# Two heads-blocks transposed by DMA instead of TensorE, later visits of the second batch, and a re-use of the score buffers, in a fused sigmoid-attention and ReGLU kernel

## The chip, the cores and the metric

The kernel runs on one core of one Trainium2 chip. The metric is the device time in microseconds (us). A core has TensorE (PE; its weight loads are listed apart as PEld), VectorE (DVE), ScalarE (ACT), GpSimd (POOL) and SyncE (SP), and 16 DMA engines that all transfers share. TensorE's results go to PSUM, eight banks of 2 KB in each of 128 partitions; VectorE and ScalarE take them from there into SBUF. Each engine works through its own instructions in order, and waits on semaphores for the others.

## What is computed

Sigmoid attention over 8 batches, 12 heads, 448 positions and 64 values a head, then a feed-forward layer (FFN) with a gate, from 768 to 1536 and back. All is float32 at the borders.

```python
scores = scale * np.matmul(q, k.transpose(0, 1, 3, 2)) - np.log(S)
attn = 1.0 / (1.0 + np.exp(-scores))
x = np.matmul(attn, v).transpose(0, 2, 1, 3).reshape(B * S, H * D)
gate = np.maximum(x @ w_gate, 0.0)
out = (gate * (x @ w_val)) @ w_out
```

## The kernel before

**Blocks and passes.** Four heads of one batch form a block; there are three blocks a batch and 24 in all (n = 0 to 23). A block's keys are cut into seven chunks of 64. One chunk of one block is a pass (168 passes): `scores` issues four matmuls of 64x64 by 448 into a PSUM tile of two banks, and one sigmoid on ScalarE turns that into `PT` (line 181). `values` then sums the seven chunks of a block against v into another two-bank tile (line 195), and two evictions make two `xT` tiles of it, VectorE's (line 211) for block 0, 1 and the first half of 2, ScalarE's (line 209) for the others. Six xT tiles are one batch's input to the FFN.

**FFN.** For each batch, `up` (twelve times) takes six matmuls for the gate and six for the value (line 230); VectorE applies the ReLU into `gate_sb` (line 247) and multiplies into `hT` (line 254). `down` (line 269) takes 128 rows of the result at a time, a part of 512 and a part of 256 columns, twelve matmuls each; VectorE scales them into `ysb` (line 283), and SyncE stores them (line 289). The first batch has three blocks of 128 rows. In the very last block, the second part is cut once more into two halves of 128 columns, in two PSUM tiles, evicted by ScalarE and VectorE.

**PSUM.** Two pools: `qkp`, three tiles of two banks, for scores, for values and for some transposes, and `wkp`, two tiles of one bank, for gate, value and down, for other transposes, and for the fillers. Fillers are matmuls with zeros at the start. They go into `fill` tiles of `wkp` (line 357).

**How q and k become operands.** They are loaded in float32, 128 rows by 896 values a block, cast to fp16 (line 105), and transposed. There are three routes. Blocks 0 to 3 go over TensorE into a `wkp` tile and over VectorE into `kT` and `qT` (line 163). Blocks 4 and 5 go the same way through a `qkp` tile (line 154); `feed` calls that after the fifth chunk (c == 4) of the block before. Blocks 6 to 23 are transposed by DMA, issued by SyncE (line 144): k, then q. The pool of kT and qT tiles has four, so that a block's tiles take the place of those of two blocks earlier.

**Who casts.** VectorE and ScalarE cast q and k of block 0, VectorE those of blocks 1 to 3, GpSimd all later ones (q first, then k, then v), and every v; GpSimd also casts the weights (line 137).

**The order of the work.** It is written out by hand. The program's order is each engine's order. A prologue runs passes 0 to 20 (batch 0). Loads that are not for blocks 0 to 2 come from one list, `order`. `start_next` takes the next item, issues its load on SyncE and its cast on GpSimd. Items are halves of the weights (g for the gate, u for the value, o for the output, three groups each) and the blocks 3, 4 and 5. Two items are taken before the passes, one in each pass from 11 to 20, and the others one at every eighth step of the first FFN. A weight load waits until one of five staging buffers has been cast.

In the FFN of batch b the passes of batch b+1 are dealt out as visits of three. The loop adds up the planned time of each step of `ffn` (0.189 us for an up matmul, columns/2400 + 0.002 for a down matmul); `todo` holds the times at which visits fall due, evenly spaced from `lo` to the end. There are eight visits in the first FFN, seven in the others. A visit issues its three passes; where a block's sigmoids are complete, it issues the values of that block ahead of its third pass; then `feed` is called for each pass. For blocks from 6 on, `feed` issues the casts at the block's predecessor's first chunk, and at its fourth chunk the DMA transposes and the load of the block after.

```python
if todo and t >= todo[0]:
    todo.pop(0)
    visit()
```

Of the kernel before, what the change touches and what calls it, by code (L numbers as in the profile page):

```python
# [9 lines left out]
FP32 = mybir.dt.float32  # L10
# [6 lines left out]
def kernel(  # L17
# [10 lines left out]
    nc = tc.nc  # L28
# [3 lines left out]
    P = 128  # L32
    HB = 4
    NBLK = H // HB
    NB = B * NBLK
    KC = 64
    NCH = S // KC
# [47 lines left out]
    def load_block(n: int, *which):  # L85
        b, i = divmod(n, NBLK)
        for nm, src, c0, c1, eng in which:
            st = stp.tile([P, 2, S], FP32, tag="st", name=f"st_{nm}")
            rows = src[b, i * HB : (i + 1) * HB].rearrange("(r h) (p c) d -> (h p) r (c d)", h=2, c=NCH)
            eng.dma_start(st[:, :, c0 * D : c1 * D], rows[:, :, c0 * D : c1 * D])  # L90
            staged[nm, n] = st

    def load_all(n: int):
        load_block(n, ("k", k, 0, NCH, nc.sync), ("q", q, 0, NCH, nc.sync), ("v", v, 0, NCH, nc.sync))

    def cast_qk(n: int, nm: str, *engines, cut=(0, NCH)):
        st = staged.pop((nm, n))
# [87 lines left out]
            qkT.pop(("k", n))  # L185

    def values(n: int, chunks):
        if chunks[0] == 0:
            PT[n] = qkp.tile([P, 2, 512], FP32, tag="qk", name="pv_ps")
        pv = PT[n]  # L190
        t = v16[n]
        for c in chunks:
            pt = PT.pop((n, c))
            for pr, r, o in ((0, 0, 0), (0, 64, 64), (1, 64, 0), (1, 0, 64)):
                nc.tensor.matmul(  # L195
                    pv[o : o + 64, pr, 0:S],
                    t[r : r + 64, pr, c * D : (c + 1) * D],
                    pt[r : r + 64, pr, :],
                    start=(c == 0),
                    stop=(c == NCH - 1),  # L200
                    tile_position=(r, o),
                    skip_group_check=True,
                )
        if chunks[-1] == NCH - 1:
            b, i = divmod(n, NBLK)
            for pr in range(2):
                x = xTp.tile([P, S], FP16, tag="xT", name="xT")
                if n >= NBLK or (pr and n == NBLK - 1):
                    nc.scalar.activation(x[:], pv[:, pr, 0:S], AF.Copy, scale=XSCALE)  # L209
                else:  # L210
                    nc.vector.tensor_scalar(  # L211
                        out=x[:], in0=pv[:, pr, 0:S], scalar1=XSCALE, scalar2=None, op0=AOP.mult
                    )
                xT[b, 2 * i + pr] = x
            PT.pop(n)
            v16.pop(n)
# [40 lines left out]
    def down(col0: int):  # L257
        o = col0 % (NHALF * S)
        ysb = ysbp.tile([P, DM], FP32, tag="ysb", name="ysb")
        last = col0 + P == B * S  # L260
        for m0, mn in ((0, 512), (512, DM - 512)):

            nb = 2 if last and m0 else 1
            w = mn // nb
            ys = [wkp.tile([P, 512], FP32, tag="wk", name="y_ps") for _ in range(nb)]
            for f in range(NFC):
                for j, y in enumerate(ys):
                    c0 = m0 + j * w
                    nc.tensor.matmul(  # L269
                        y[:, 0:w],  # L270
                        hT[f][:, o : o + P],
                        wo[f // FG][:, f % FG, c0 : c0 + w],
                        start=(f == 0),
                        stop=(f == NFC - 1),
                    )
                if f < NFC - 1:
                    yield mn / 2400.0 + 0.002
            for j, y in enumerate(ys):
                dst = ysb[:, m0 + j * w : m0 + (j + 1) * w]
                if nb == 2 and j == 0:  # L280
                    nc.scalar.activation(dst, y[:, 0:w], AF.Copy, scale=OUT_SCALE)  # L281
                else:
                    nc.vector.tensor_scalar(out=dst, in0=y[:, 0:w], scalar1=OUT_SCALE, scalar2=None, op0=AOP.mult)  # L283
            if last or m0 + mn == DM:
                s0 = m0 if last else 0
                for half, eng in enumerate((nc.sync, nc.scalar if last else nc.sync)):
                    b, r = divmod(col0 + 64 * half, S)
                    rows = out[b * S : (b + 1) * S].rearrange("(p c) m -> c p m", c=NCH)
                    eng.dma_start(rows[r // KC][:, s0 : m0 + mn], ysb[64 * half : 64 * half + 64, s0 : m0 + mn])
            yield mn / 2400.0 + 0.002  # L290
# [5 lines left out]
    def ffn(b: int):  # L296
        for f in range(NFC):
            if b == 0 and f == 0:
                yield from up(b, f, 4, 4)
            else:  # L300
                yield from up(b, f)
        for col0 in blocks128(b):
            yield from down(col0)
# [12 lines left out]
    def feed(i: int):  # L316

        n, c = divmod(i, NCH)
        m = n + 1
        if c == 0 and NPRO <= m < NB:  # L320
            cast_block(m)
        if c == 4 and NBLK < m < NPRO:
            transposes(m, "k")
            transposes(m, "q")
        if c == 3 and NPRO <= m < NB:
            dma_transposes(m)
        if c == 3 and NPRO <= m + 1 < NB:
            load_all(m + 1)

    valued: set = set()  # L330
    state = {"pass": NBLK * NCH}
    def visit():
# [16 lines left out]

    zeros = const.tile([P, 512], FP16, name="zeros")  # L350
    nc.vector.memset(zeros[:], 0.0)
    fill: list = []

    def filler(*widths):

        for w in widths:
            nc.tensor.matmul(fill[-1][:, 0:w], zeros[:, 0:P], zeros[:, 0:w], start=True, stop=True)

    def new_fill():
        fill.append(wkp.tile([P, 512], FP32, tag="wk", name="fill"))  # L360

    with tc.manual_schedule():
        nc.scalar.activation(warm[:], bias_t[:], AF.Sigmoid)  # L363
# [6 lines left out]
        def halves(kind, j):  # L370
            return [(kind, j, 0), (kind, j, 1)]

        order = halves("g", 0) + [3] + halves("u", 0) + halves("g", 1) + halves("u", 1)
        order += [4] + halves("g", 2) + halves("u", 2) + halves("o", 0) + [5]
        order += halves("o", 1) + halves("o", 2)

        def start_next():
            what = order.pop(0)
            if isinstance(what, int):
                load_all(what)  # L380
                if what > NBLK:
                    cast_block(what)
                else:
                    cast_v(what, nc.gpsimd)
            else:
                load_w(*what)
                cast_w(*what, nc.gpsimd)

        new_fill()
        filler(*[512] * 10)  # L390
        cast_qk(0, "q", nc.vector, nc.scalar, cut=(0, 4, NCH))
        cast_qk(0, "k", nc.vector, nc.scalar, cut=(0, 2, 4))
        transposes(0, "q")
        filler(128, 128)
        transposes(0, "k", nc.scalar, nc.vector, cut=(0, 2, 4))
        new_fill()
        filler(128, 128, 128)
        cast_qk(0, "k2", nc.vector, cut=(4, NCH))
        for n in range(NBLK):
# [7 lines left out]
        for i in range(NP0 + 2):  # L407
            n, c = divmod(i, NCH)
            if n < NBLK:
                scores(n, c)  # L410
            while done <= i - (4 if i < NP0 - 4 else 2):
                values(done // NCH, [done % NCH])
                done += 1
            if i == 2:
                qk16["k", 0] = qk16.pop(("k2", 0))
                transposes(0, "k", nc.vector, cut=(4, NCH))
            if 1 <= i <= 3:
                filler(256)
            if c == 1 and n + 1 < NBLK:
                cast_qk(n + 1, "k", nc.vector)  # L420
                cast_qk(n + 1, "q", nc.vector)
            if c in (3, 5) and n + 1 < NBLK:
                transposes(n + 1, "k" if c == 3 else "q")
            if i == 14:
                cast_qk(NBLK, "k", nc.vector)
            if i == 15:
                transposes(NBLK, "k")
                cast_qk(NBLK, "q", nc.vector)
            if i == 16:
                transposes(NBLK, "q")  # L430
            if i in (18, 21):
                gv_part(0, 0, wg, [0, 1] if i == 18 else [2, 3])
            if 11 <= i < NP0:
                start_next()

        for b in range(B):
            total = ffn_us(b)
            todo = []
            if b + 1 < B:
                count = NBLK * NCH // 3 + (1 if b == 0 else 0)  # L440
                lo = 6.0 if b == 0 else 0.0
                todo = [lo + (k + 0.5) * (total - lo) / count for k in range(count)]
            t = 0.0
            for step, cost in enumerate(ffn(b)):
                t += cost
                if order and step % 8 == 0:
                    start_next()
                if todo and t >= todo[0]:
                    todo.pop(0)
                    visit()  # L450
            for _ in todo:
                visit()

# [28 lines left out]
```

## Time and profile before

| what | value |
|---|---|
| median of 8 runs | 433.89 us (433.37 to 435.44) |
| the profiled execution | 434.65 us |
| its span, first to last instruction | 432.9 us |
| TensorE matmul busy | 418.9 us, 97% |
| VectorE / ScalarE / GpSimd busy | 166.0 / 178.7 / 103.2 us |
| up matmuls (line 230), 1152 | 254.9 us |
| down matmuls (line 269), 684 | 113.8 us |
| scores (line 171) and values (line 195), 672 each | 49.1 and 39.3 us |
| transposes on TensorE (line 157), 84 | 7.5 us |
| DMA transposes (line 144), 36 | 3.0 to 3.1 us from issue to landing |
| DMA, mean over the span | 155 GB/s |

Times in the profile are us from the start of the span. A row of a group gives the busy time, the mean of one in ns, and the idle time ahead of it with what ended it. Matmuls are pipelined and their ends are modelled, so that neighbours overlap in the records; the distance between starts is the better measure. The span leaves out 1.75 us that the execution's time includes.

### The profile page before, as it was taken

The numbers are of one execution on the slowest core, as the hardware profiler recorded it, in microseconds if no ns is written. First come the engines' busy times: TensorE is split into PE (matmuls) and PEld (weight loads), VectorE is DVE, ScalarE is ACT, GpSimd is POOL, SyncE is SP. The second block draws the span as 40 slices with busy tenths as digits, with TensorE's granted clock in tenths as the row PEclk, the third lists the DMA queues.
The fourth block names the chain that finished last, engine by engine and source line by source line (L and its number), as shares of the span: only waits on it lengthen the run. The fifth ranks groups of instructions, "written<-read, shape, count | busy, mean of one in ns | idle before, by whom it ended". The sixth has DMA issues, their size and how long they took to land.

```text
span 432.9 us, 7873 instructions
## 1 busy us (share of the span) xinstructions
PE 418.9 (97%) x3282; PEld 216.2 (50%) x3282; DVE 166.0 (38%) x276; ACT 178.7 (41%) x217; POOL 103.2 (24%) x137
## 2 busy tenths in 40 slices
PE   6879899999999999999999999999999999999996
PEld 3334455545455455554455454554455544555553
DVE  3535442244323533243522444234432445235531
ACT  5862445553534353525254435252534352500000
POOL 2667783233110333003230133103330030000000
PEclk9899999999999999999999999999999999999998
DMA  8999997365624754296432765156454630030014
GB/s 305 383 386 385 392 355 196 83 180 164 171 74 102 184 151 148 75 186 192 99 110 73 207 171 170 47 110 183 135 151 111 156 94 0 18 94 0 2 36 109
DMA packets 64371, 66.96 MB, mean 155 GB/s; under 512 B 35792, under 2 KB 54608, under 8 KB 64336
## 3 DMA queue, kind: packets, MB, share of 16 engines
q1 hardware_dynamic: 63088, 64.63, 51.4%
q10 hardware_dynamic: 1248, 1.84, 1.2%
q8 instruction: 25, 0.41, 0.4%
q14 instruction: 10, 0.08, 0.1%
HBM read 47.19 MB, written 11.01 MB: 134 GB/s over the span
## 4 chain that ended last, share of the span: by engine, by line
PE 92%; ACT 3%; DMA 2%; DVE 1%; issue 1%; ACTq 0%; DVEq 0%
PE gv_ps L230 51%; PE y_ps L269 26%; PE qk_ps L171 8%; PE pv_ps L195 7%; ACT PT L181 3%; DMA st_q<-in_q_dram 2%; PE tr L157 1%; ACT xT L209 0%; DVE h16q L105 0%; DVE ysb L283 0%; DVE gate_sb L247 0%; DVE xT L211 0%; ACT L363 0%; ACTq L90 0%; DVE kT L163 0%
## 5 line engine op out<-in xcount | busy, mean ns | idle before, releaser
L181 ACT ACTIVATE PT<-qk_ps,bias_t 128x896 f16<-128x896 f32 x168 | 159.4, 1008 | 196.1 <-PE qk_ps L171 196.1
L230 PE MATMUL gv_ps<-xT,wg 128*128 128x448 f16 x576 | 128.1, 353 | 0.6 <-DVE gate_sb L247 0.3
L230 PE MATMUL gv_ps<-xT,wv 128*128 128x448 f16 x576 | 126.8, 353 | 0.0
L269 PE MATMUL y_ps<-wo,hT 128*128 128x512 f16 (+2 forms) x684 | 113.8, 324 | 0.7 <-DVE ysb L283 0.7
L269 PEld LDWEIGHTS <-hT 128*128 128x128 f16 x684 | 64.5, 98 | 48.9 <-issue 7.2
L247 DVE TENSOR_SCALAR gate_sb<-gv_ps 128x448 f32<-128x448 f32 x96 | 60.0, 625 | 71.9 <-PE gv_ps L230 71.9
L254 DVE TENSOR_TENSOR hT<-gate_sb,gv_ps 128x448 f16<-128x448 f32 x96 | 59.6, 621 | 63.4 <-PE gv_ps L230 63.1
L230 PEld LDWEIGHTS <-wv 128*128 128x128 f16 x576 | 55.1, 98 | 55.1 <-issue 5.7
L230 PEld LDWEIGHTS <-wg 128*128 128x128 f16 x576 | 55.0, 98 | 55.0 <-issue 6.5
L105 POOL CAST h16q<-st_q 128x896 f16<-128x896 f32 x20 | 18.6, 930 | 223.8 <-DMA st_q<-in_q_dram 199.8
L283 DVE TENSOR_SCALAR ysb<-y_ps 128x512 f32<-128x512 f32 (+2 forms) x56 | 31.1, 556 | 105.7 <-PE y_ps L269 105.7
L171 PE MATMUL qk_ps<-qT,kT 64*64 64x448 f16 x672 | 49.1, 362 | 2.0 <-ACT PT L181 1.7
L195 PE MATMUL pv_ps<-PT,v 64*64 64x448 f16 x672 | 39.3, 353 | 0.9 <-ACT PT L181 0.8
L171 PEld LDWEIGHTS <-kT 64*64 64x64 f16 x672 | 16.1, 106 | 28.0 <-issue 22.2
L195 PEld LDWEIGHTS <-v 64*64 64x64 f16 x672 | 20.1, 108 | 13.0 <-issue 2.3
L209 ACT ACTIVATE xT<-pv_ps 128x448 f16<-128x448 f32 x43 | 21.0, 547 | 6.0 <-PE pv_ps L195 4.8
L281 ACT ACTIVATE ysb<-y_ps 128x128 f32<-128x128 f32 x1 | 0.3, 277 | 45.4 <-PE y_ps L269 45.4
L105 POOL CAST h16k<-st_k 128x896 f16<-128x896 f32 x20 | 18.6, 928 | 0.0
L112 POOL CAST v<-st_v 128x448 f16<-128x448 f32 x24 | 13.4, 556 | 14.4 <-DMA st_v<-in_v_dram 14.4
L113 POOL CAST v<-st_v 64x448 f16<-64x448 f32 x24 | 13.9, 580 | 1.5
L114 POOL CAST v<-st_v 64x448 f16<-64x448 f32 x24 | 13.6, 568 | 1.0
L137 POOL CAST wv<-st_wu 128x1536 f16<-128x1536 f32 x6 | 8.8, 1466 | 2.7 <-DMA st_wu<-in_moe_w_val_dram 2.7
(26 smaller groups left out, 57.5 us busy)
## 6 DMA issues: line engine op xcount, KB each, us to landing
out_dram<-ysb SPq DMA_DIRECT2D x54, 192.0 KB, 2.7
st_q<-in_q_dram SPq DMA_DIRECT2D x23, 448.0 KB, 4.6
st_v<-in_v_dram SPq DMA_DIRECT2D x23, 448.0 KB, 5.3
st_k<-in_k_dram SPq DMA_DIRECT2D x22, 448.0 KB, 4.0
st_wg<-in_moe_w_gate_dram SPq DMA_DIRECT2D x6, 768.0 KB, 11.9
st_wu<-in_moe_w_val_dram SPq DMA_DIRECT2D x6, 768.0 KB, 12.7
st_wo<-in_moe_w_out_dram SPq DMA_DIRECT2D x6, 768.0 KB, 11.8
st_v<-in_v_dram ACTq DMA_DIRECT2D x1, 448.0 KB, 5.5
```

The costliest lines, as they stand in the source:

```text
L105: eng.tensor_copy(o, i)
L113: eng.tensor_copy(t[0:64, 1], st[64:128, 1])
L114: eng.tensor_copy(t[64:128, 1], st[0:64, 1])
L171: nc.tensor.matmul(ps[o : o + 64, bank, 0:S], kT[r : r + 64, c, h, :], qT[r : r + 64, :, h, :], start=True, stop=True, tile_position=(r, o ...
L181: nc.scalar.activation(pt[:], ps[:, :, 0:S], AF.Sigmoid, bias=bias_t[:], scale=qk_scale)
L195: nc.tensor.matmul(pv[o : o + 64, pr, 0:S], t[r : r + 64, pr, c * D : (c + 1) * D], pt[r : r + 64, pr, :], start=(c == 0), stop=(c == NCH ...
L209: nc.scalar.activation(x[:], pv[:, pr, 0:S], AF.Copy, scale=XSCALE)
L230: nc.tensor.matmul(begun[key][:, 0:S], w[j][:, dc, jj * P : (jj + 1) * P], xT[b, dc][:], start=(dc == 0), stop=(dc == NDC - 1),)
L247: nc.vector.tensor_scalar(out=g_sb[:], in0=gate[:, 0:S], scalar1=0.0, scalar2=None, op0=AOP.max)
L254: nc.vector.tensor_tensor(out=hT[f][:, o : o + S], in0=g_sb[:], in1=val[:, 0:S], op=AOP.mult)
L269: nc.tensor.matmul(y[:, 0:w], hT[f][:, o : o + P], wo[f // FG][:, f % FG, c0 : c0 + w], start=(f == 0), stop=(f == NFC - 1),)
L283: nc.vector.tensor_scalar(out=dst, in0=y[:, 0:w], scalar1=OUT_SCALE, scalar2=None, op0=AOP.mult)
```

## The change

1. **Blocks 4 and 5.** `feed` no longer transposes them on TensorE. `order` has two new items, -4 and -5, for which `start_next` calls `dma_transposes`: block 4 after the second half of u2 and ahead of o0, block 5 at the very end, after the last half of w_out. A list `later`, with a loop to take from it, is added too; nothing is ever put into it.
2. **Block 3.** Its v is loaded after u0, not with its k and q. Its casts on VectorE move from passes 14 and 15 to 15 and 17, its transposes on TensorE from 15 and 16 to 17 and 20.
3. **Visits.** In the first FFN `lo` is 10.0, not 6.0: the first visit falls due later and the eight stand closer together.
4. **PSUM.** The fillers write into the tile of block 0's values, taken from `qkp` at the start, not into tiles of `wkp`. The two halves of the last down block take the two banks of one `qkp` tile.
5. **First up step.** Three, not four, of the value matmuls of the first FFN group run ahead of the gate's last two.

```diff
     def values(n: int, chunks):
-        if chunks[0] == 0:
+        if chunks[0] == 0 and n not in PT:
             PT[n] = qkp.tile([P, 2, 512], FP32, tag="qk", name="pv_ps")
...
-            ys = [wkp.tile([P, 512], FP32, tag="wk", name="y_ps") for _ in range(nb)]
+            if nb == 2:
+                yt = qkp.tile([P, 2, 512], FP32, tag="qk", name="y_ps")
+                ys = [yt[:, 0], yt[:, 1]]
+            else:
+                ys = [wkp.tile([P, 512], FP32, tag="wk", name="y_ps")]
...
-                yield from up(b, f, 4, 4)
+                yield from up(b, f, 4, 3)
...
-        if c == 4 and NBLK < m < NPRO:
-            transposes(m, "k")
-            transposes(m, "q")
...
+    later: list = []
...
+        if 0 not in PT:
+            PT[0] = qkp.tile([P, 2, 512], FP32, tag="qk", name="pv_ps")
         for w in widths:
-            nc.tensor.matmul(fill[-1][:, 0:w], zeros[:, 0:P], zeros[:, 0:w], start=True, stop=True)
+            nc.tensor.matmul(PT[0][:, 0, 0:w], zeros[:, 0:P], zeros[:, 0:w], start=True, stop=True)
...
-        order = halves("g", 0) + [3] + halves("u", 0) + halves("g", 1) + halves("u", 1)
-        order += [4] + halves("g", 2) + halves("u", 2) + halves("o", 0) + [5]
-        order += halves("o", 1) + halves("o", 2)
+        order = halves("g", 0) + ["kq"] + halves("u", 0) + ["v"] + halves("g", 1) + halves("u", 1)
+        order += [4] + halves("g", 2) + halves("u", 2) + [-4] + halves("o", 0) + [5]
+        order += halves("o", 1) + halves("o", 2) + [-5]
...
             what = order.pop(0)
-            if isinstance(what, int):
+            if isinstance(what, int) and what < 0:
+                dma_transposes(-what)
+            elif isinstance(what, int):
                 load_all(what)
-                if what > NBLK:
-                    cast_block(what)
-                else:
-                    cast_v(what, nc.gpsimd)
+                cast_block(what)
+            elif isinstance(what, str):
+                load_all(NBLK, what)
+                if what == "v":
+                    cast_v(NBLK, nc.gpsimd)
...
-            if i == 14:
+            if i == 15:
                 cast_qk(NBLK, "k", nc.vector)
-            if i == 15:
+            if i == 17:
+                cast_qk(NBLK, "q", nc.vector)
                 transposes(NBLK, "k")
-                cast_qk(NBLK, "q", nc.vector)
-            if i == 16:
-                transposes(NBLK, "q")
             if i in (18, 21):
                 gv_part(0, 0, wg, [0, 1] if i == 18 else [2, 3])
+            if i == 20:
+                transposes(NBLK, "q")
...
-                lo = 6.0 if b == 0 else 0.0
+                lo = 10.0 if b == 0 else 0.0
...
-                    todo.pop(0)
+                    due = todo.pop(0) + 2.0
                     visit()
+                if later and t >= due:
+                    m = later.pop(0)
+                    transposes(m, "k")
+                    transposes(m, "q")
```

More of the change, by code (lines that the diff above doesn't have):

```diff
@@ L91, in load_block, with load_all @@
             staged[nm, n] = st
-    def load_all(n: int):
-        load_block(n, ("k", k, 0, NCH, nc.sync), ("q", q, 0, NCH, nc.sync), ("v", v, 0, NCH, nc.sync))
+    def load_all(n: int, names="kqv"):
+        for nm, src in (("k", k), ("q", q), ("v", v)):
+            if nm in names:
+                load_block(n, (nm, src, 0, NCH, nc.sync))
     def cast_qk(n: int, nm: str, *engines, cut=(0, NCH)):
@@ L351 @@
     nc.vector.memset(zeros[:], 0.0)
-    fill: list = []
     def filler(*widths):
+        if 0 not in PT:
+            PT[0] = qkp.tile([P, 2, 512], FP32, tag="qk", name="pv_ps")
         for w in widths:
-            nc.tensor.matmul(fill[-1][:, 0:w], zeros[:, 0:P], zeros[:, 0:w], start=True, stop=True)
-    def new_fill():
-        fill.append(wkp.tile([P, 512], FP32, tag="wk", name="fill"))
+            nc.tensor.matmul(PT[0][:, 0, 0:w], zeros[:, 0:P], zeros[:, 0:w], start=True, stop=True)
     with tc.manual_schedule():
@@ L387, in start_next @@
                 cast_w(*what, nc.gpsimd)
-        new_fill()
         filler(*[512] * 10)
@@ L395 @@
         transposes(0, "k", nc.scalar, nc.vector, cut=(0, 2, 4))
-        new_fill()
         filler(128, 128, 128)
```

## The prediction

> **What bounds the kernel now.** I read the page's busy times first, then the chain that ended last, then the busy time by windows, and last the timelines of SyncE's queue and of GpSimd.
>
> ```profile
> PE 418.9 (97%) x3282; PEld 216.2 (50%) x3282; DVE 166.0 (38%) x276; ACT 178.7 (41%) x217; POOL 103.2 (24%) x137
> ...
> DMA  8999997365624754296432765156454630030014
> ```
>
> TensorE sets the time, but the DMA row says that the first six slices (0 to 65 us) are a second regime: the transfer engines are full there. The chain around the places that the change touches, in order of time (start, length, what):
>
> ```profile
> 45.05 0.72 PE qk_ps L171 x12
> 45.77 0.02 issue
> 45.79 0.02 ACTq L181
> 45.80 0.57 issue
> 46.38 1.01 ACT PT L181
> 47.38 0.04 issue
> 47.43 0.55 PE tr L157 x7
> 47.98 4.16 PE gv_ps L230 x22
> ```
>
> Between the scores and the next FFN matmul lie 47.98 - 45.77 = 2.21 us: TensorE transposes block 4, each in a buffer of the scores' pool that a sigmoid must free first. For block 5 the chain resumes at 60.71 where the last scores ended at 58.77 (58.58 + 0.19, the spacing of one pass): 1.94 us. Busy time by windows (length, then PE, PEld, DVE, ACT, POOL busy, clock, DMA share, GB/s):
>
> ```profile
> 7.38:10.80 3.42, 1.18 (x16) 0.74 (x13) 1.52 (x3) 3.08 (x4) 1.25 (x3) 1.00 1.06 388
> 10.80:14.20 3.40, 3.40 (x34) 1.79 (x35) 0.84 (x2) 1.90 (x2) 1.77 (x4) 0.50 1.06 383
> ```
>
> ```profile
> 59.00:62.00 3.00, 2.39 (x22) 1.60 (x22) 1.75 (x3) 2.00 (x4) 2.37 (x2) 1.00 1.04 383
> 62.00:65.00 3.00, 3.00 (x20) 1.42 (x21) 1.46 (x4) 0.00 (x0) 1.68 (x2) 1.00 0.67 241
> ...
> 97.00:99.70 2.70, 2.70 (x16) 1.37 (x14) 1.40 (x3) 0.00 (x0) 0.52 (x1) 1.00 0.91 170
> ```
>
> The DMA share is 1.04 or more until 62 and falls only after. The last line holds one pair of DMA transposes (block 8's, issued 95.82 and 97.14) and nothing else: 0.91 of 2.70 us. GpSimd's timeline says when the last weights land:
>
> ```profile
> 62.40 1.47 POOL L137 CAST wo<-st_wo 128x1536 f16<-128x1536 f32 x1 [0.54 <-DMA st_wo<-in_moe_w_out_dram]
> 64.78 0.93 POOL L105 CAST h16q<-st_q 128x896 f16<-128x896 f32 x1 [0.92 <-DMA st_q<-in_q_dram]
> ```
>
> So the last half of w_out lands at about 62.35, and everything put into SyncE's queue behind it lands later still.
>
> **What the skill says.** The Trainium skill, "DMA: Bandwidth & Descriptors", section "Queues, rings and completion order": each issuing engine owns one ring on each of the 16 transfer engines, and descriptors are consumed in ring order. The trace agrees as far as it goes: all of SyncE's transfers, transposes too, stand in one queue (q1). "Advanced Engine Details and Errata", section "X-Bar Transpose (TRN2)", calls transposes "as fast as regular DMAs". Here the trace differs: 0.91 x 2.70 = 2.46 us of all engines for 2 x 128 x 896 x 2 B = 459 KB, at 170 GB/s in the window where loads run at 383; I use 2.46. "TensorE: Matmul & The Clock Gate", section "Part 1: The HAM clock gate", says that about 3.4 us of idleness halves the clock until about 3.4 us of activity restores it. The trace agrees: the window 7.38 to 10.80, with 1.18 us busy, is followed by 3.4 us at 0.50.
>
> **The change part by part.**
>
> Removed from TensorE: the transposes of blocks 4 and 5, 2.21 + 1.94 = -4.15 us, and four DVE copies that lay beside matmuls (0).
>
> Added to SyncE and DMA, block 4: the pair goes behind the loads of u2 and ahead of o0. It waits for GpSimd's cast of k, which ended at 39.6; o0's first load, issued at 36.81 before, goes out at about 39.7 + 2 x 1.3 = 42.3. The DMA does not run dry: u2 lands only at 47.0 (GpSimd's wait). The pair then takes 2.46 us of a full DMA, lands near 47.0 + 2.46 + 0.5 = 49.9, and every later load is 2.46 us late. Its first user, pass 28, comes in the third visit, about 51 to 52.5: no wait, with some 1.5 us to spare.
>
> Block 5: its pair is the last thing that start_next issues, behind all of w_out. It waits for kT3 and qT3 to be free (pass 27, in the same third visit) and for the cast of k, 55.2 + 2.46 = 57.7. Neither is what comes last: the ring is full until 62.35 + 2.46 = 64.8, then the pair takes 2.46 (67.3), and its completion comes about 0.3 us later after its last packet than a load's does (issue of q to landing 3.0, packets ending 2.5 after issue). It lands at about 67.5.
>
> Its first user is pass 35. Visits: 38.88 us planned, lo = 10, 8 visits, so they fall due at 11.8, 15.4, 19.0, 22.6 and 26.2. The up stage ends at (5 + 11 x 12) x 0.189 = 25.9, so four visits precede the down stage instead of five, and the fifth, with passes 33, 34, 35, comes after two of the first block's matmuls. TensorE gets there early: before, the first down matmul began at 66.64; less 4.15, less one visit (0.69), plus 0.43 and two passes (0.39) gives 62.6, and up to 1.3 less for what the start gains. It then stands at pass 35 for 5 to 6 us, and with it everything behind it on TensorE, all of the FFN.
>
> The sum is made from that wait. Before, 15 down matmuls ended at 69.72, and what followed took 432.9 - 69.72. After: 67.5 + 0.1 (start) + 0.19 (pass 35) + 2.45 (13 matmuls left: 10 x 0.213 + 3 x 0.107) = 70.24, or +0.5 us. So the wait eats the 4.15 and the visit moved out of its way.
>
> The clock: 5 to 6 us of stand hold a whole window with little work, so TensorE restarts at half. It stays there for 1.7 to 5.1 us (to the end of the first sufficiently busy window), each costing half: 0.9 to 2.6. I take +1.7. Where the stand is shorter than 3.4 us this is nothing.
>
> Tail: the last block's two halves come out of the scores' pool. The chain now has PE, DVE ysb 0.70, PE; the second matmul of that stretch started at 427.99 where 427.10 was possible: -0.89. But two engines then read one tile. In the first value tile (xT of block 2) ScalarE waited for VectorE to finish reading the other bank (1.1 us), so the last VectorE eviction goes behind ScalarE's 0.28: net -0.6.
>
> Hidden by the wait, whatever they give: casts and transposes of block 3 later (TensorE waited 0.89 at 24.31 for the cast of q, ScalarE idled 0.80: up to -0.8); fillers into the first value tile (the first passes have two buffers instead of three, third scores at 7.7 instead of 7.05, while sigmoids fill 6.76 to 10.46 either way: 0; two fewer work tiles may let block 1's transposes start up to 1 us before 10.65: 0 to -1). v of block 3 behind u0: the same bytes, u0 a load (some 1.2 us) earlier: 0. One matmul of the first value projection moved behind the gate: it fills TensorE's 0.34 us wait for VectorE's gate_sb at 32.55: 0. If the block 5 wait did not exist, these would be worth -1 to -2.
>
> Further on: block 6 loads behind block 5's pair, lands near 69.5 instead of 64.8, is cast by 73, transposed by 75.5; its pass 42 comes at about 82. No wait.
>
> Sum: +0.5 + 1.7 - 0.6 = +1.6 us on the profiled span of 432.9. That execution took 434.65, 1.75 around the span; the median of the runs is 433.89, so I forecast 435.5.
>
> **What is not in the trace.** It shows no transpose behind a backlog of loads. Bounds: from 0 per pair, if they slip in without taking anything, to about 4 us if short packets of 256 B suffer between large ones. I take 2.46.
>
> **Rivals.** (1) The stand is shorter, or the clock holds: the pairs cost 2 us each, or the restart falls early in a window. Then -0.1 to +0.9: 434.0, no change. For it: packets overlap in a full queue (share 1.04). Against it: the stand is still about 5 us. (2) Faster: the transposes are not held behind the loads. If block 5's pair lands by about 62.6, pass 35 does not wait, and the next limit is the last w_out half, cast by 63.9, wanted for the eleventh down matmul at 68.8 before and near 64.6 now. Gain 4.2 to 4.9 and the tail 0.6: 428.5 to 429. It decides at one point: with a cold restart the change breaks even when the pair lands at 65.9, without it at 67.6. For it: the skill's equal speed (459 KB at 383 GB/s is 1.2 us, landing near 65.1). Against: the measured 170 GB/s and one queue. (3) Transposes behind loads take some 4 us per pair: block 4 also comes late (51.5), block 5 lands near 70.6: 438.5. (4) The change doesn't do what it says: its list of later transposes is never filled, so nothing happens there; the DMA route alone is live.
>
> **Numbers.** The forecast 0.58 (435.5, its own range 434.3 to 437.2), rival 1 0.14 (434.0), rival 2 0.14 (428.5 to 433), rival 3 0.14 (438.5). The list that stays empty alters no time. Leaving out most of rival 2 and the upper part of rival 3 gives 432.6 to 438.4. About 0.2% (0.9 us) is what a measurement can tell here. Of the forecast's 0.58 some 0.05 lies within it; with rival 1 the chances are faster 0.14, same 0.19, slower 0.67.
>
> **What would show it.** Right: block 5's DMA transposes landing at 66.5 to 68.5; a wait of 4 us or more of TensorE at L171 for them, at about 62; 0.5 of clock after it; the last w_out cast near 64.9; no tr after block 3; the stretch at 427 gone, and ScalarE's eviction ahead of VectorE's at the end. Wrong: the pair landing before 65, which makes it faster; a wait at pass 28 for block 4; a wait for the weights in the first down block.

## The result, and the profile after

The changed kernel takes 436.85 us (median of 11 runs, 436.22 to 437.56), the kernel before 433.98 (32 runs): a ratio of 1.0065, 95% interval 1.0056 to 1.0075. It is slower by 2.9 us. The profiled execution has a span of 434.9 us.

TensorE's total of busy time hardly shows it. From the page of the changed kernel, TensorE's and the scores' rows (busy and mean; then idle time ahead of the row and what ended most of it):

```profile
PE 418.8 (96%) x3254; PEld 214.9 (49%) x3254; DVE 164.5 (38%) x272; ACT 178.5 (41%) x217; POOL 102.4 (24%) x137
...
L173 PE MATMUL qk_ps<-qT,kT 64*64 64x448 f16 x672 | 49.0, 360 | 9.5 <-DMA qT<-h16q 5.8
```

28 matmuls are gone from TensorE, and the scores' matmuls now wait 5.8 us for one transfer. The chain that ended last (start, length, what) shows that wait in the middle of the visit with passes 33 to 35:

```profile
30.31 11.13 PE gv_ps L232 x58
...
50.23 0.69 PE qk_ps L173 x12
...
56.63 3.34 PE gv_ps L232 x17
59.97 0.02 issue
59.99 0.20 DVE hT L256
60.19 6.37 DMA qT<-h16q
66.56 0.14 issue
66.69 0.59 PE qk_ps L173 x4
67.28 5.73 PE y_ps L275 x23
```

The third visit, at 50.2, has pass 28, block 4's first: no wait. Block 5's operands land at 66.56, and pass 35 begins at 66.69. The windows around it (length, then PE, PEld, DVE, ACT, POOL busy, clock, DMA share, GB/s):

```profile
59.00:62.00 3.00, 1.89 (x16) 0.63 (x13) 1.10 (x2) 1.19 (x2) 2.91 (x3) 1.00 1.03 399
62.00:65.00 3.00, 0.00 (x0) 0.00 (x0) 0.00 (x0) 0.72 (x1) 2.00 (x2) 0.89 1.15 270
65.00:66.50 1.50, 0.00 (x0) 0.00 (x0) 0.00 (x0) 0.00 (x0) 1.47 (x1) 0.50 1.22 314
66.50:70.00 3.50, 3.31 (x11) 1.18 (x12) 0.00 (x0) 1.01 (x1) 0.84 (x1) 0.50 0.96 341
70.00:74.00 4.00, 4.00 (x41) 2.31 (x43) 1.12 (x2) 0.56 (x1) 2.58 (x5) 0.85 0.00 0
```

TensorE stands, the clock is halved at 64.36, and it comes back at 71.18, two windows of 3.41 us later; TensorE works in 4.5 us of that. The DMA stays full until the pair has landed. SyncE's queue (start, time in issuing) and GpSimd's last weight cast:

```profile
39.30 1.33 SPq L146 DMA_TRANSPOSE kT<-h16k  x1
40.69 5.26 SPq L146 DMA_TRANSPOSE qT<-h16q  x1
46.00 1.09 SPq L125 DMA_DIRECT2D st_wo<-in_moe_w_out_dram  x2
...
57.89 2.21 SPq L146 DMA_TRANSPOSE kT<-h16k  x1
60.19 3.29 SPq L146 DMA_TRANSPOSE qT<-h16q  x1
```

```profile
65.02 1.47 POOL L139 CAST wo<-st_wo 128x1536 f16<-128x1536 f32 x1 [0.53 <-DMA st_wo<-in_moe_w_out_dram]
```

The last weights come 65.02 - 62.40 = 2.62 us later than before. That is block 4's pair: the same cast begins at 62.35 in e1_tensor_route, which has neither pair, and at 65.11 in e3_no_transpose_5, which has block 4's alone. Block 5's own pair lands 1.5 us after this cast begins. By the packets in the trace it ran from 63.1 to 66.1, so that part of it lay beside the last loads.

The start is better than before. ScalarE's sigmoids run almost without a gap, and the first FFN's first ReLU begins at 29.63, not at 31.87.

### The profile page after: what moved, and what is told of

Its sections match the earlier page's. It is cut to its first block, busy times and chain, and to the rows that moved or that the text cites. A ratio compares the mean times of both kernels' runs of the same rounds, so it can differ in the third digit from the quotient of the medians.

```text
span 434.9 us, 7815 instructions
## 1 busy us (share of the span) xinstructions
PE 418.8 (96%) x3254; PEld 214.9 (49%) x3254; DVE 164.5 (38%) x272; ACT 178.5 (41%) x217; POOL 102.4 (24%) x137
## 4 chain that ended last, share of the span: by engine, by line
PE 93%; ACT 4%; DMA 1%; DVE 1%; issue 0%; ACTq 0%
PE gv_ps L232 51%; PE y_ps L275 26%; PE qk_ps L173 8%; PE pv_ps L197 7%; ACT PT L183 3%; DMA qT<-h16q 1%; PE pv_ps L362 1%; PE tr L159 0%; DVE ysb L289 0%; DVE gate_sb L249 0%; DVE xT L213 0%; ACT xT L211 0%; ACTq L295 0%; ACT kT L163 0%; ACT ysb L287 0%
## 5 line engine op out<-in xcount | busy, mean ns | idle before, releaser
L275 PE MATMUL y_ps<-wo,hT 128*128 128x512 f16 (+2 forms) x684 | 115.8, 327 | 0.0
```

The costliest lines, as they stand in the source:

```text
L275: nc.tensor.matmul(y[:, 0:w], hT[f][:, o : o + P], wo[f // FG][:, f % FG, c0 : c0 + w], start=(f == 0), stop=(f == NFC - 1),)
```

## The experiments

The kernels were measured in three sets: e1_tensor_route, e2_kept_warm, e3_no_transpose_5 and e4_tail_as_before; then c_changed (the changed kernel again, as a control) with the runs e5, e6 and e8; then c2_changed (the same) with e2b, e7 and e9. Ratios are to the kernel before, whose median in the sets was 433.76, 433.74 and 433.85 us. The first set has no such control; its runs are held against the 436.85, 437.03 and 436.93 us that the changed kernel took in the result and in the other two sets.

**The DMA route undone (e1_tensor_route).**

```diff
-        order += [4] + halves("g", 2) + halves("u", 2) + [-4] + halves("o", 0) + [5]
-        order += halves("o", 1) + halves("o", 2) + [-5]
+        order += [4] + halves("g", 2) + halves("u", 2) + halves("o", 0) + [5]
+        order += halves("o", 1) + halves("o", 2)
...
+        if c == 4 and NBLK < m < NPRO:
+            transposes(m, "k")
+            transposes(m, "q")
```

> The changed kernel with blocks 4 and 5 transposed on TensorE again, at their old place in the order of work; the items -4 and -5 are gone, all else as changed. Theory (the wait at pass 35 for block 5's DMA transposes, and the half clock after it, are what the change costs): TensorE pays the 4.15 us of before again, but the wait is gone and the first FFN still begins 2.2 us earlier than before (27.9 against 30.1), the tail gives 0.1: 433.98 - 2.3 = 431.7 us. Rival (the later visits, or the new use of the score buffers, cost the time): 434 or more, as these are kept.

Measured: 432.11 us, ratio 0.9958 (0.9943 to 0.9972). With all the other edits kept, the kernel is faster than before, by 1.65 us in its set. So the DMA route costs some 4.8 us more than the route over TensorE at its old place. The later visits and the new use of the score buffers are not what makes the changed kernel slower; what the visits and the first up step give by themselves was not measured. The chain of e1_tensor_route shows the transposes' price unchanged, 48.71 - 46.50 = 2.21 us for block 4:

```profile
45.78 0.72 PE qk_ps L173 x12
46.50 0.02 issue
46.52 0.02 ACTq L183
46.53 0.57 issue
47.11 1.01 ACT PT L183
48.12 0.04 issue
48.16 0.55 PE tr L159 x7
48.71 3.68 PE gv_ps L232 x19
```

**The stand filled, so that the clock stays (e2_kept_warm, and e2b_kept_warm beside the changed kernel in one set).**

```diff
+            if i == 35:
+                wt = wkp.tile([P, 512], FP32, tag="wk", name="warm_ps")
+                for _ in range(25):
+                    nc.tensor.matmul(wt[:], zeros[:, 0:P], zeros[:], start=True, stop=True)
             scores(*divmod(i, NCH))
```

> The changed kernel with 25 matmuls of zeros (512 columns, 5.4 us at full clock) ahead of pass 35, where TensorE stands. Theory (a stand of 5.8 us and then some 4.5 us at half clock): the fillers fit into the stand, the clock stays at 1.00, and the time falls by about 2.2 us: 434.6 us. Rival (the half clock costs nothing, since TensorE would wait behind it anyway, for weights or stores): 436.5 to 437 us, with the clock at 1.00 as well.

> The kernel of e2_kept_warm again, now beside the changed kernel in one set. Theory (half clock over 4.5 us of work behind the stand): 1.7 to 2.3 us less than c2_changed. Rival (the clock is worth nothing there): the same as c2_changed.

> The changed kernel once more, as the control of this set. Theory: 436.8 to 437.3 us.

Measured: 435.37 us (1.0037, 1.0024 to 1.0050) in the first set; in the third 435.49 (1.0028, 1.0018 to 1.0038) beside 436.93 (1.0064, 1.0042 to 1.0086) for the changed kernel. Keeping the clock up gives 1.4 us, less than the 1.7 to 2.3 expected. On the work behind the stand alone it gives more. TensorE's timeline of e2b_kept_warm:

```profile
61.07 5.57 PE L348 MATMUL warm_ps<-zeros 128*128 128x512 f16 x25
68.34 0.38 PE L173 MATMUL qk_ps<-qT,kT 64*64 64x448 f16 x4 [1.71 <-DMA qT<-h16q]
68.66 3.86 PE L275 MATMUL y_ps<-wo,hT 128*128 128x512 f16 x23
72.44 0.57 PE L173 MATMUL qk_ps<-qT,kT 64*64 64x448 f16 x8
```

From pass 35 to the next visit it takes 72.44 - 68.34 = 4.10 us at full clock. For the same work c2_changed takes 5.88 us (67.16 to 73.04), the profiled changed kernel 6.26 (66.69 to 72.95) and c_changed 6.56 (66.75 to 73.31). So half clock costs 1.8 to 2.5 us. But the operands landed 1.2 us later in e2b_kept_warm than in its control (68.34 against 67.16), and 0.6 later in the first set than in e4_tail_as_before (67.84 against 67.23). That eats the difference. It is the transfers that are slower beside the fillers: from 65.0 to 66.5 the DMA moved 23 GB/s in e2b_kept_warm and 245 in its control, and the last half of w_out is late as well (its cast begins at 66.70, not 65.50). Why was not settled.

**Block 5's pair left out (e3_no_transpose_5).**

```diff
+            if what == -5:
+                for nm in ("k", "q"):
+                    qk16.pop((nm, 5))
+                    qkT[nm, 5] = qkT[nm, 4]
-            if isinstance(what, int) and what < 0:
+            elif isinstance(what, int) and what < 0:
                 dma_transposes(-what)
```

> The changed kernel without block 5's pair of DMA transposes: the scores of block 5 read block 4's operands instead, so its results are another's; everything else is issued as in the changed kernel. Theory: pass 35 no longer waits; TensorE goes on to the ninth and eleventh matmul of the first down block, whose weights are cast by 64.5 and 66.5, and stands there for 2 to 3 us, with some half clock: 432.5 us (431.4 to 433.5). Rival (not this pair holds TensorE at 61 to 67): 436.5 to 437 us.

Measured: 434.68 us (432.28 to 435.98 over 20 runs), ratio 1.0020 (1.0009 to 1.0030). The wait at pass 35 is gone, and the next limit is the one named: from the table of waits,

```profile
PE y_ps L275 <- POOL wo L139: 3.1, 3, 1.4
```

three waits, 3.1 us, for the last halves of w_out. The size was missed by 2 us. The profiled execution, at clock 1.000, took 432.28, as expected; the others had mean clocks of 0.992 to 0.996, and took 434.1 to 436.0. A window of 3.41 us at half clock lowers the mean by 0.004, so they lost one or two. It is likely that they lost them at these waits, since the kernels with the same start and without the waits (e1_tensor_route, e5_later, e6_later_tail) have 0.998 or more in 11 of 12 executions; no trace of a slower execution shows it. So leaving out this one pair gives 2.2 us in the median and 4.6 at full clock: the wait for the pair makes way for the waits for weights that the first pair has delayed, and mostly for half clock again.

**The same pair ahead of the last weights (e8_pair_before_o2), with the control c_changed.**

```diff
-        order += halves("o", 1) + halves("o", 2) + [-5]
+        order += halves("o", 1) + [-5] + halves("o", 2)
```

> The changed kernel with block 5's pair of DMA transposes ahead of the last two loads of w_out, not behind them. Theory (the DMA is full up to that point, so the pair's 2.5 us fall on whatever comes last in it): pass 35 begins near 63.5 to 64, but the last w_out halves are then cast near 66 and 68, and the ninth and eleventh matmul of the first down block wait for them; the clock is halved as well: 434.5 to 436.5 us. Rival (only the pair's place behind the weights is at fault): the wait at pass 35 shrinks by 4 us and no other comes: 432 to 433 us.

> The changed kernel itself, as a control beside the others of this set. Theory: 436.8 to 437.3 us, pass 35 beginning at 66.7 to 67.8 as block 5's pair lands, then half clock for one or two windows of 3.4 us.

Measured: 437.06 us (434.99 to 437.48), ratio 1.0061 (1.0041 to 1.0082), no different from the control's 437.03 (1.0069, 1.0054 to 1.0084); the expected 434.5 to 436.5 was a little low. TensorE's timeline of e8_pair_before_o2, and two of its windows:

```profile
63.07 0.38 PE L173 MATMUL qk_ps<-qT,kT 64*64 64x448 f16 x4 [2.00 <-DMA qT<-h16q]
63.38 2.65 PE L275 MATMUL y_ps<-wo,hT 128*128 128x512 f16 x6
66.93 1.01 PE L275 MATMUL y_ps<-wo,hT 128*128 128x512 f16 x2 [0.90 <-POOL wo L139]
68.90 4.00 PE L275 MATMUL y_ps<-wo,hT 128*128 128x512 f16 x15 [0.95 <-POOL wo L139]
```

```profile
60.00:63.50 3.50, 1.50 (x16) 0.47 (x15) 0.62 (x1) 1.91 (x2) 2.46 (x2) 1.00 1.01 237
63.50:67.00 3.50, 2.60 (x7) 0.80 (x6) 0.00 (x0) 1.01 (x1) 1.47 (x1) 0.50 1.03 384
```

The wait for the pair falls from 5.6 us in the control to 2.0, and two waits for w_out take its place, at the ninth and eleventh matmul of the block; the clock is at half for three windows, from 63.5 to 73.8. So the place behind the weights is not the fault. The DMA is full until it has brought all that the first down block needs, and a pair ahead of the weights makes them later: block 4's by 2.6 us, block 5's here by 2.3 (the last cast begins at 67.38, in c_changed at 65.07).

**The tail (e4_tail_as_before).**

```diff
-            if nb == 2:
-                yt = qkp.tile([P, 2, 512], FP32, tag="qk", name="y_ps")
-                ys = [yt[:, 0], yt[:, 1]]
-            else:
-                ys = [wkp.tile([P, 512], FP32, tag="wk", name="y_ps")]
+            ys = [wkp.tile([P, 512], FP32, tag="wk", name="y_ps") for _ in range(nb)]
```

> The changed kernel with the last down block's two halves in two tiles of the work pool, as before. The prediction gave that part -0.6 us, so this would be 437.4; the traces give it -0.1 (from the last 512-column matmul to the end 6.07 us before, 5.98 after), so this should be 436.9 to 437.0. What decides: whether the 0.9 us that TensorE saves there is given back by ScalarE, which issues a store of its own before it may evict.

Measured: 437.82 us, ratio 1.0090 (1.0074 to 1.0107); the changed kernel has 436.85, 437.03 and 436.93, in other sets. The difference of 0.8 to 1.0 is more than the prediction's -0.6 for this part, and far from the -0.1 that I read from two traces. But the operands for pass 35 landed 0.5 us later in this trace, which is not the tail's doing. From the last 512-column matmul to the end it is 6.31 us here and 5.95 in the changed kernel. To the issue of the last store alone it is 3.03 us here and before, and 2.65 in the changed kernel. What follows, 3.02 to 3.30 us, differs between traces of kernels that end alike, and by that the two traces had misled. So the part helps, by 0.4 us as the traces have it; whether the rest of the difference is its own is open. How, the changed kernel's timeline shows:

```profile
429.34 0.69 DVE L289 TENSOR_SCALAR ysb<-y_ps 128x512 f32<-128x512 f32 x1 [2.17 <-PE y_ps L275]
430.06 0.55 ACTq L295 DMA_DIRECT2D out_dram<-ysb  x1
430.94 0.28 ACT L287 ACTIVATE ysb<-y_ps 128x128 f32<-128x128 f32 x1 [44.85 <-PE y_ps L275]
431.25 0.29 DVE L289 TENSOR_SCALAR ysb<-y_ps 128x128 f32<-128x128 f32 x1 [1.22 <-ACT ysb L287]
```

TensorE's wait is gone, but ScalarE has its own store ahead in its queue, which waits for VectorE's 0.69 us and takes 0.55 to issue; then VectorE waits 1.22 us for ScalarE. Both read one tile; in e6_later_tail below, with two tiles, VectorE waits for TensorE and no longer for ScalarE.

**The transposes on TensorE, but later (e5_later, e6_later_tail).** The change added a list for this and never filled it. e5_later takes the two items out of `order`, as e1_tensor_route does, and fills the list:

```diff
+        if c == 4 and NBLK < m < NPRO:
+            later.append(m)
```

> The changed kernel with blocks 4 and 5 on TensorE again, by the list that the change added and left empty: each block's transposes run at the first step 2 us of planned time after the visit that has chunk 4 of the block before; items -4 and -5 are gone. Theory (of the 4.15 us that the transposes cost before, some 1.6 are 28 matmuls of 0.055 us, the rest waits for score buffers that a sigmoid still reads; 2 us later these are free): 2.4 less than at the old place (432.11), so 429.7 us. Rival (the waits move along): 432.

Measured: 429.85 us, ratio 0.991 (0.989 to 0.993): faster than before by 3.9 us and than the changed kernel by 7, as expected. TensorE's timeline:

```profile
48.38 0.55 PE L159 MATMUL tr<-ident,h16k 128*128 128x128 f16 x7
48.77 0.55 PE L159 MATMUL tr<-ident,h16q 128*128 128x128 f16 x7
49.16 0.54 PE L232 MATMUL gv_ps<-xT,wg 128*128 128x448 f16 x2
```

The 14 transposes of a block take 49.16 - 48.38 = 0.78 us, with no wait ahead of them, where they cost 2.21 at the old place. The waits did not move along. e6_later_tail also splits the last two halves into two tiles and issues the first part's two stores on SyncE:

```diff
-                yt = qkp.tile([P, 2, 512], FP32, tag="qk", name="y_ps")
-                ys = [yt[:, 0], yt[:, 1]]
+                ys = [qkp.tile([P, 2, 512], FP32, tag="qk", name="y_ps")[:, 0] for _ in range(2)]
...
-            for half, eng in enumerate((nc.sync, nc.scalar if last else nc.sync)):
+            for half, eng in enumerate((nc.sync, nc.scalar if last and m0 else nc.sync)):
```

> As e5_later, and at the end the two halves of the last down block in two separate tiles of the scores' pool, with the first part's two stores both issued by SyncE, so that ScalarE's eviction waits neither for its own store nor VectorE's for ScalarE's. Theory: the evictions follow TensorE's last matmul at once, 0.6 us less than e5_later: 429.1 us. Rival (the end is set by the stores that are already on their way): no difference to e5_later.

Measured: 429.72 us, ratio 0.990 (0.9885 to 0.9915), no different from e5_later, as the rival had it. The evictions do follow at once, but SyncE issues two stores before its last one. That is issued 2.65 us after the last 512-column matmul in e5_later (424.81 less 422.16), and still 2.35 after it in e6_later_tail (424.81 less 422.46). The part that was freed is partly given back in that queue.

**The start, part by part, on the kernel before (e7_fillers_alone, e9_block3_alone).** The first moves only the fillers, the second only block 3's casts and transposes.

```diff
-            nc.tensor.matmul(fill[-1][:, 0:w], zeros[:, 0:P], zeros[:, 0:w], start=True, stop=True)
+            nc.tensor.matmul(PT[0][:, 0, 0:w], zeros[:, 0:P], zeros[:, 0:w], start=True, stop=True)
```

> The kernel before with only the fillers moved into the value tile of block 0. Theory (the fillers' tiles kept block 1's transposes of k waiting until 10.65, and what followed ran at half clock): ScalarE's first gap of 1.6 us goes, the first FFN begins 1 to 1.5 us earlier, nothing later takes it back: 432.5 to 433.0 us. Rival (two score buffers in place of three at the start cost as much): 433.5 to 434.

```diff
-            if i == 14:
-                cast_qk(NBLK, "k", nc.vector)
...
-                transposes(NBLK, "k")
+                cast_qk(NBLK, "k", nc.vector)
+            if i == 17:
...
-            if i == 16:
-                transposes(NBLK, "q")
+                transposes(NBLK, "k")
...
+            if i == 20:
+                transposes(NBLK, "q")
```

> The kernel before with only block 3's casts and transposes later (casts at passes 15 and 17, transposes at 17 and 20). Theory (they take away ScalarE's gap of 0.80 us at 24.5): 432.9 to 433.2 us. Rival (the gap moves to another pass): 433.7.

Measured: 433.52 us (0.9984, 0.9973 to 0.9995) and 433.61 (0.9987, 0.9973 to 1.0001). The medians are 0.3 and 0.2 us lower, and the second one's interval still touches no change. Both were expected to give more; the first lies in its rival's range, the second between its theory and its rival. The medians mix two kinds of execution, though. Those with a mean clock of 0.997 or more have a median span of 431.8 us before, 431.6 with the fillers moved and 431.0 with block 3 later. So among these block 3 gives 0.8 us, as much as the gap that was to go. A lower mean clock was seen in 24 of 47 executions before, in 6 of 12 with block 3 later, and in 2 of 18 with the fillers moved: what the moved fillers give seems to be that a window at half clock is lost more seldom. The profile of before had misled: it is of an execution that ran 3.4 us at half clock at the start. In the first set, executions of the kernel before with a mean clock of 1.000 had spans of 431.7 to 431.8, those at 0.994 or 0.995 mostly 432.6 to 432.8; the profiled one is at 0.993 with 432.9. The start's gain against an execution that loses no window is about 1 us smaller than against that one.

## Why the prediction was right

The direction and the place were right, and the time, 436.85 us, lies within 434.3 to 437.2, near its upper end. By its steps:

- **Block 4's pair hidden, at the price of later loads: right.** No wait at pass 28. The last w_out cast was to be near 64.9 and began at 65.02.
- **Block 5's pair last in the queue, landing at 67.5: right in kind.** It landed at 66.56; in the controls pass 35 began at 66.75 and 67.16. The estimate of 2.46 us for block 4's pair fits the 2.62 measured. Block 5's pair was taken to start when the last weights had come, and to land 2.7 us after them; its packets began beside theirs, and it landed some 1.5 us after them.
- **A stand of 5 to 6 us at pass 35: right**, 5.8 us, though by luck in part: it ended 0.9 us early, and TensorE came to it at 60.9, where 62.6 less up to 1.3 was forecast. e1_tensor_route showed that this route costs the time, e8_pair_before_o2 and e3_no_transpose_5 that the limit behind it is the DMA's load and not its order.
- **Half clock, +1.7: a little small.** 2.16 us in the profiled execution (6.26 less 4.10), 1.8 and 2.5 in the controls. That a stand shorter than 3.4 us costs nothing is wrong: in e8_pair_before_o2 the clock was halved after one of 2.0 us.
- **The work from pass 35 on at full clock: 0.3 too little.** The sum gives 0.19 + 2.45 us to the fifteenth matmul, and 1.2 more for the ten to the visit (one of 0.216 and nine of 0.109); e2b_kept_warm takes 4.10.
- **The tail, -0.6: a little much.** It is -0.4 to the issue of the last store. The order of ScalarE before VectorE was right; that ScalarE's own store stands ahead of its eviction was overlooked.
- **The start hidden by the wait: right.** It begins the FFN 2.2 us earlier in the profiles, and the total shows none of it, as TensorE only waits longer.

On the profiled span these leave little: 434.5 forecast (432.9 + 1.6), 434.9 measured. -0.9 for the landing, +0.46 for the clock, +0.5 for the tail as these two spans have it and +0.3 for the work add up to +0.4. That the landing came early while the other terms were too low is luck; the mechanism didn't need it. The larger part of the miss, 435.5 against 436.85, is the last step: **the difference was worked out against one execution (434.65) and then laid on the median (433.89).** That is right where both kernels' ends hang on the same thing. Here the end of the changed kernel hangs on a landing, while the end of the kernel before follows its start, and the profiled one had lost a window at half clock there. Laid on 434.65 the same sum gives 436.25. That the clock at the start doesn't move the landing is argued, not tested.

Rival 1 failed, as the clock was halved. Rival 2, the faster one, needed block 5's pair by about 62.6; its packets began only at 63.1, behind the loads in the queue. The limit that it named next, the last half of w_out, is the one that e3_no_transpose_5 then met. Rival 3 came nearer than it seemed: in the full queue block 4's pair took from 44.5 to 47.7, 3.2 us, by its packets, though the loads behind it lost only 2.6. Of rival 4, the list that stays empty is indeed without effect; filled, it makes e5_later 2.3 us faster than e1_tensor_route. One reading was off without consequence: the DMA share is 1.03 from 56 to 59, not 1.04 or more.

## What to carry to other kernels

Moving work off the engine that sets the total can gain nothing where the resource that takes it is full and has to bring what that engine needs next. Here the DMA is full for the first 62 us. A pair of transposes, 2.46 us of DMA time on an empty queue, made the last weights, and what stood behind them, 2.6 us later, some three times what the same transposes cost TensorE (0.78 us) once they were put where their buffers are free. Before a step is moved, ask whether its price at the old place is its work or its waits; here the waits, 1.4 us for block 4 and 1.2 for block 5, were got rid of by a shift of 2 us. And a stand on TensorE can cost more than its length: here half clock behind it added 1.8 to 2.5 us.

## What was not expected of the hardware

- Issuing a DMA transpose takes 1.3 us when the queue is empty (1.31 at 74.6), and 5.26 and 3.29 us (the pairs' second halves; the first took 1.33 and 2.21) when it is full. SyncE's next load went out at 46.0, not at 42.3 as forecast. The DMA didn't run dry by that: its share was 1.26 from 44 to 47 and 1.04 from 47 to 50.
- No whole idle window is needed for half clock, as one could think from the prediction. Before, 1.18 us of work in 3.42 was too little; in e8_pair_before_o2, half clock followed 3.5 us with 1.50 of work, whose longest stand was 2.0. Nor does little work in any such stretch suffice: in the profiled execution of e3_no_transpose_5 the clock stayed at full over 3.5 us with 0.96 of work (63.5 to 67.0). It seems to matter how the stretch lies to the windows, which would also explain why the other executions fared differently; that was not tested.
- A kernel with short stands can scatter: e3_no_transpose_5 ranges over 3.7 us, with the mean clock falling from 1.000 to 0.992 along with it.
